# The order of a score tile and a product in the 64-row dense part of a fused attention and gated MLP kernel

## The chip, the cores and the metric

One Trainium2 chip, one of its cores. A core has TensorE (matmuls; PE in the profile, its weight loads are PEld), VectorE (DVE), ScalarE (ACT), GpSimd (POOL), SyncE (SP) and DMA queues; each engine works through its own queue, and they wait for each other by semaphores. TensorE writes to PSUM, which has eight banks; a matmul of 512 float32 columns fills one. The metric is the device time of one execution in microseconds (us), the median of some runs.

## What is computed

```python
xn = layernorm(x)                                   # x: 2048 x 512
q, k, v = xn @ wqkv, in 32 heads of 16
p = softmax(q @ k.T / 4)                            # per head, 2048 x 2048
s = (p @ v, heads joined) @ wo
g = silu(gelu(xn @ w1 + b1) @ w2 + b2)              # 512 -> 1376 -> 512
out = x + s * g
```

All in float32. The kernel gets float32 accuracy from the faster fp32r matmuls by splitting an operand into a high and a low part: a product is three matmuls, high x high, high x low and low x high.

## The kernel before

The program is one long, hand-ordered queue for each engine. It has three parts.

The first normalizes x, turns it, and makes the first columns of q, k and v.

The second is the **64-row dense part**. Here the remaining columns of q, k, v and all of the MLP are computed. Contractions of 128 rows are cut into two halves: a matmul takes rows 0 to 63 (row half 0) or 64 to 127 (row half 1) of its operands, and two matmuls of different halves can be in TensorE together. `run` (lines 593 to 600) gets two lists of such matmuls, one for each half, and queues them in pairs: `mm` (562 to 575, the matmul is at line 569) places one product of half `a`. An accumulation is begun by one half and ended by the other; `mark` (579 to 585, a tiny ACT or DVE copy) and the counters `prog`, `writer` and `seen` see to it that the second half begins on a bank only when the first is done.

In the same part **score tiles** are computed ahead of the attention, for the row maxima that the softmax needs: 128 queries against 512 keys of one head, a matmul of 48 rows on one row half (`s_mm`, line 190). `fill` (546 to 554) decides, before each product of half `a`, whether a score of that half goes in: when the half's count of matmuls, `row[a]`, has reached `due`, when it is that half's turn (`made`), and as long as fewer than 4 x LEAD = 604 have been placed. `due` grows by about three matmuls for each score, so that half 0 gets one, half 1 one three pairs later, half 0 the next two pairs after that: each half has a score and five products in turn. `taken` (556 to 560) counts the score.

A score takes one of two PSUM banks in turn (`s_ring`, line 91, and `s_tile`), and VectorE reads it with one maximum over each half of the 512 columns (`s_max`, line 195). So a score has to wait until the maximum of the score before the last has read its bank. When a block of 64 scores is done, `s_end0` (line 250) and `s_end1` (line 269) add a small maximum and a transpose on VectorE. The other banks hold accumulations of the dense part, which ACT empties (lines 363, 365, 382, 656).

The third part does the attention: transposed scores and exponentials (`t_one`), sums and products with v (`pv_step`), the rest of the score tiles (`s_op`), and at last the output projection and the gate.

What is queued where in the dense part is written out by `plan` (a list of dense halves and second-layer parts, made by due counts); each of its steps calls `run`. The order inside a pair is the loop in `run`, shown in the diff.

Of the kernel before, what the change touches and what calls it, by code (L numbers as in the profile page):

```python
# [49 lines left out]
def fused(ctx: ExitStack, tc: tile.TileContext, x, wqk, wv, wo, w1, b1, w2, b2, out):  # L50
# [115 lines left out]
    def tick():  # L166
        for e in later:
            e[0] -= 1
# [40 lines left out]
    def s_one(a):  # L209
        made[a] += 1  # L210
        s_whole(heads[made[a] - 1], a)
# [55 lines left out]
    def s_end1(u):  # L267
        mh = qring.tile([P, 2 * GH * NCH], F32, name="mh", bufs=1)
        nc.vector.transpose(mh, NM.pop(u).rearrange("p i a -> p (i a)").bitcast(F32))
        nc.sync.dma_start(mh_d[u].rearrange("i j (q b s) -> b (i j q) s", b=NCH, s=2 * GH * NCH), mh)  # L270
        sent.add(u)
# [274 lines left out]
    def fill(a):  # L546
        due = FILL0 + sum(made) * ROWS // (4 * LEAD)
        if sum(made) < 4 * LEAD and row[a] >= due and (made[0] <= made[1]) == (a == 0):
            taken()
            if later and later[0][0] <= 0:  # L550
                s_end1(later.pop(0)[1])
            s_one(a)
            row[a] += 1
            tick()

    def taken():
        prog["pe"] += 1
        s_when.append(prog["pe"])
        if len(s_when) > 2:
            prog["seen"] = max(prog["seen"], s_when[-3])  # L560

    def mm(a, key, ps, lhs, rhs, first, last):
        r = slice(64 * a, 64 * a + 64)
        token = None
        if not first and writer[key][0] != a and writer[key][1] > prog["seen"]:
            if not tokens or tokens[-1][0] < writer[key][1]:
                mark()
            prog["seen"], token = next(x for x in tokens if x[0] >= writer[key][1])
        i = nc.tensor.matmul(ps, lhs[r], rhs[r], start=first, stop=last).ins  # L569
        if token is not None:  # L570
            tc.add_manual_dep(i, token, SYNC, reason="other row tile")
        prog["pe"] += 1
        row[a] += 1
        latest[0] = (prog["pe"], i.name)
        writer[key] = (a, prog["pe"])
# [3 lines left out]
    def mark(dve=False):  # L579
        if dve:  # L580
            i = nc.vector.tensor_copy(junk[:, 1:], ident_r[:1, :1].bitcast(F32)).ins
        else:
            i = nc.scalar.activation(junk[:, :1], ident_r[:1, :1].bitcast(F32), AF.Copy).ins  # L583
        tc.add_manual_dep(i, latest[0][1], SYNC, reason="row tile done")
        tokens.append((latest[0][0], i.name))
# [7 lines left out]
    def run(ops, hooks={}):  # L593
        for n, two in enumerate(zip(*ops)):
            prog["n"] += 1
            for a in range(2):
                fill(a)
                mm(a, *two[a])
            for h in hooks.get(n, []):
                h()  # L600
# [25 lines left out]
    def down(c, f, part):  # L626
# [13 lines left out]
        if (c, f, part) == parts[-2]:  # L640
            run(ops, {2: [lambda: mark(True)], 5: [lambda: mark(True)]})
        else:
            run(ops, {3: [lambda: mark_early(n)]})
# [30 lines left out]
    def half(j, h):  # L674
        x, y = pairs[j]
        if h == 0:
            PH[x] = ps_x.tile([P, CH], F32, name="ps")
            PH[y] = ps_m.tile([P, CH], F32, name="ps")
            run((terms(x, 0, True), terms(y, 1, True)), {4: [lambda: w1_split(j + 1)], 8: [errand], 10: [chore]})
        else:  # L680
            run((terms(y, 0, False), terms(x, 1, False)), {2: [lambda: w1_load(j + 2), errand], 10: [chore]})
            evac((x, y), PH)
# [385 lines left out]
```

## Time and profile before

| what | value |
| --- | --- |
| median of 3 runs | 1564.38 us (1564.31 to 1565.07) |
| the profiled execution | 1565.26 us, its span 1563.2 us |
| first part, 0 to 41.66 us | PE busy 37.25, DVE 31.69, ACT 19.07 of 41.66 |
| dense part, 41.66 to 479.24 us | PE busy 437.58, DVE 395.19, ACT 167.71 of 437.58 |
| attention and output, 479.24 to the end | PE busy 1078.94, DVE 963.42, ACT 1055.35 of 1083.92 |
| granted TensorE clock | 1.00 in all three |

The span runs from the first to the last instruction of the program in the profile; the execution's own time is a little longer. A busy time is the time in which at least one instruction of the engine was running; two overlapping matmuls count once. In the prediction's fences, a timeline row gives start, length, engine, line, operation, tiles (written <- read) and shapes; L190 is a score, L569 a product, L195 the maximum that reads a score.

### The profile page before, as it was taken

What the parts mean: (1) busy time and instruction counts of PE and PEld (TensorE: products, weight loads), DVE (VectorE), ACT (ScalarE), POOL (GpSimd) and SP (SyncE); (2) the same over time, 40 slices, a digit from 0 to 9 for tenths busy, and PEclk for the clock granted to TensorE, in tenths of its full rate; (3) what the DMA queues carried; (4) which work ended last, traced back from release to release, by engine and by line L of the source; (5) the groups of instructions that cost most, each with busy time, mean ns of one, the idle gap of its engine ahead of it and who ended that gap; (6) DMA issues with size and microseconds to landing.
All of it is one profiled execution on the core that took longest, in us unless ns stands there. A gap on an engine that the chain in (4) does not pass through costs nothing.

```text
span 1563.2 us, 32584 instructions
## 1 busy us (share of the span) xinstructions
PE 1553.8 (99%) x12254; PEld 959.4 (61%) x12254; DVE 1390.3 (89%) x2306; ACT 1242.1 (79%) x2487; POOL 374.0 (24%) x392
## 2 busy tenths in 40 slices
PE   8999999999999999999999999999999999999998
PEld 7899999999995444444444444444444444444456
DVE  7899999999998999999999999999999999999833
ACT  4333343434348999999999999999999999999994
POOL 4135574755752000000000100010110000000144
PEclk9999999999999999999999999999999999999999
DMA  7515343356435011311110411141141111110153
GB/s 218 159 47 139 113 158 108 114 140 155 138 96 116 21 42 37 67 30 30 39 33 22 70 30 39 40 72 45 36 68 34 31 31 30 38 35 20 49 188 125
DMA packets 79501, 117.38 MB, mean 75 GB/s; under 512 B 28876, under 2 KB 29132, under 8 KB 77968
## 3 DMA queue, kind: packets, MB, share of 16 engines
q1 hardware_dynamic: 75884, 102.36, 23.7%
q0 software_dynamic: 2976, 12.35, 4.3%
q8 instruction: 97, 1.59, 0.4%
q10 hardware_dynamic: 484, 0.60, 0.1%
q14 instruction: 60, 0.49, 0.1%
HBM read 84.81 MB, written 25.97 MB: 71 GB/s over the span
## 4 chain that ended last, share of the span: by engine, by line
PE 98%; DVE 1%; DMA 1%; ACT 0%; issue 0%; ACTq 0%; SPq 0%
PE pv L800 32%; PE pst L737 15%; PE ps L737 14%; PE ps L569 13%; PE ps L190 10%; PE pst L569 7%; PE pv L569 3%; PE ps L917 2%; PE ps L450 1%; PE ps L81 1%; PE pst L81 1%; DVE st L411 0%; DMA xt<-in_x 0%; PE pst L434 0%; DVE slot L76 0%; DVE xn L425 0%
## 5 line engine op out<-in xcount | busy, mean ns | idle before, releaser
L195 DVE TENSOR_REDUCE mx<-ps 128x2 f32<-128x512 f32 x2048 | 1298.0, 685 | 108.1 <-PE ps L190 28.8
L739 ACT ACTIVATE slot<-pst 128x512 f32<-128x512 f32 x1533 | 804.2, 606 | 2.4 <-PE ps L190 1.5
L800 PE MATMUL pv<-slot,vsb 128*17 128x512 f32 (+1 forms) x4096 | 537.5, 598 | 0.2 <-DVE os L807 0.2
L190 PE MATMUL ps<-kt,slot 48*128 48x512 f32 x1350 | 382.7, 371 | 0.0
L739 ACT ACTIVATE slot<-ps 128x512 f32<-128x512 f32 x515 | 307.7, 598 | 5.4 <-PE ps L737 1.9
L737 PE MATMUL pst<-qt,kt 50*128 50x512 f32 x1149 | 304.8, 405 | 0.1
L737 PEld LDWEIGHTS ps<-qt,kt 50*128 50x128 f32 x387 | 70.8, 183 | 316.2 <-ACT slot L739 315.1
L190 PEld LDWEIGHTS ps<-kt,slot 48*128 48x128 f32 x1350 | 223.5, 184 | 4.1 <-DVE mx L195 0.5
L569 PE MATMUL ps<-slot,w1h 64*128 64x512 f32 x1104 | 222.7, 393 | 0.0
L737 PEld LDWEIGHTS pst<-qt,kt 50*128 50x128 f32 x1149 | 207.9, 185 | 21.9 <-DVE gt L654 1.2
L737 PE MATMUL ps<-qt,kt 50*128 50x512 f32 x387 | 190.1, 493 | 0.0
L190 PE MATMUL ps<-kt,qz 48*128 48x512 f32 x448 | 187.2, 418 | 0.0
L190 PE MATMUL ps<-slot,slot 48*128 48x512 f32 x584 | 168.7, 372 | 0.0
L569 PEld LDWEIGHTS ps<-slot,w1h 64*128 64x128 f32 x1104 | 156.2, 185 | 4.9 <-ACT junk L583 0.2
L569 PE MATMUL ps<-slot,w1l 64*128 64x512 f32 x552 | 145.8, 392 | 0.0
L370 POOL TENSOR_TENSOR hl<-hg,hh 128x512 fp32r<-128x512 f32 x76 | 96.8, 1295 | 134.2 <-ACT hh L369 108.8
L800 PEld LDWEIGHTS pv<-slot,vsb 128*17 128x17 f32 (+1 forms) x4096 | 69.8, 96 | 85.5 <-issue 33.3
L583 ACT ACTIVATE junk<-ident_r 1x1 f32<-1x1 f32 x94 | 18.4, 196 | 124.0 <-PE pst L569 112.5
L737 PE MATMUL pst<-qt,slot 50*128 50x512 f32 x384 | 99.7, 405 | 0.0
L190 PEld LDWEIGHTS ps<-slot,slot 48*128 48x128 f32 x584 | 97.3, 184 | 3.5 <-DVE mx L195 1.0
L837 POOL TENSOR_TENSOR slot<-slot,dn 64x512 f32<-64x512 f32 x16 | 20.5, 1282 | 315.5 <-PE pst L737 198.8
L190 PEld LDWEIGHTS ps<-kt,qz 48*128 48x128 f32 x448 | 82.1, 183 | 15.7 <-DVE mx L195 1.0
(153 smaller groups left out, 1744.7 us busy)
## 6 DMA issues: line engine op xcount, KB each, us to landing
raw<-in_w SPq DMA_DIRECT2D x88, 256.0 KB
qk_h<-hh SPq DMA_DIRECT2D x32, 256.0 KB
qk_l<-hl SPq DMA_DIRECT2D x32, 256.0 KB
qt<-qk_h SPq DMA_DIRECT2D x128, 64.0 KB
slot<-qk_h SPq DMA_DIRECT2D x92, 64.0 KB
g_d<-gt POOLq DMA_DIRECT2D x16, 256.0 KB, 3.1
qt<-qk_l SPq DMA_DIRECT2D x64, 64.0 KB
kt<-qk_h POOLq DMA_DIRECT2D x16, 256.0 KB, 6.3
```

The costliest lines, as they stand in the source:

```text
L81: nc.tensor.matmul(ps, lhs[a], rhs[b], start=first and n == 0, stop=last and n == 2)
L190: return nc.tensor.matmul(ps[:, c0:c0 + w], QS[u][r, p, qi * P:(qi + 1) * P], keys, start=True, stop=True).ins
L195: nc.vector.tensor_reduce(MX[u][:, 2 * p:2 * p + 2, qi, ki][:, heads, parts], ps.rearrange("p (n c) -> p n c", c=HC), axis=AX.X, op=OP.max)
L370: nc.gpsimd.tensor_sub(hl, raw, hh.bitcast(F32))
L450: nc.tensor.matmul(pq["q", g, c], W1[g][i][:, k * P:(k + 1) * P], (xh, xl)[j][c][:, k], start=n == 0 and k == 0, stop=n == 2 and k == KT - 1)
L569: i = nc.tensor.matmul(ps, lhs[r], rhs[r], start=first, stop=last).ins
L583: i = nc.scalar.activation(junk[:, :1], ident_r[:1, :1].bitcast(F32), AF.Copy).ins
L737: nc.tensor.matmul(ps, kts[KSET[g]][p][r, k * P:(k + 1) * P], QT[u][r, p, :], start=True, stop=True)
L739: nc.scalar.activation(PT[u, k][:, 2 * p + a, :], ps, AF.Exp, scale=SCALE)
L800: nc.tensor.matmul(PV[u][32 * j:32 * j + w, :], vsb[:, k, h:h + w], PT[u, k][:, j, :], start=(k == 0), stop=(k == NT - 1))
L837: eng.tensor_mul(ot[c][rs, g // 2], ot[c][rs, g // 2], DN.pop(u)[rs])
L917: op = nc.tensor.matmul(PW[b][0], OTS[b, k][i][r], (wo_h, wo_l)[j][r, k], start=part == 0 and n == 0, stop=part == 3 and n == 5).ins
```

## The change

In each pair of the dense part, both calls of `fill` now come ahead of both products. Before, the queue of TensorE had, for one pair: score of half 0 (if due), product of half 0, score of half 1 (if due), product of half 1. After, it has: score of half 0 (if due), score of half 1 (if due), product of half 0, product of half 1. For half 0 nothing moves; a score of half 1 goes one place ahead.

```diff
     def run(ops, hooks={}):
         for n, two in enumerate(zip(*ops)):
             prog["n"] += 1
             for a in range(2):
                 fill(a)
+            for a in range(2):
                 mm(a, *two[a])
             for h in hooks.get(n, []):
                 h()
```

## The prediction, made before the change was run

> **What bounds the kernel now.** I read the first page for the engines and the chain of waits.
>
> ```profile
> span 1563.2 us, 32584 instructions
> ...
> PE 98%; DVE 1%; DMA 1%; ACT 0%; issue 0%; ACTq 0%; SPq 0%
> ```
>
> 98% of the chain is TensorE's own work: time taken off or put on TensorE in one stage reaches the end. Then the dense part alone, in the table by stretches: first the instructions of the product line L569, then those of the score line L190 (columns: stretch, its length, TensorE busy and count, loads busy and count, granted clock, DMA share, GB/s).
>
> ```profile
> 41.66:479.24 437.58, 437.56 (x3072) 396.48 (x3072) 1.00 0.43 123
> ```
> ```profile
> 41.66:479.24 437.58, 252.64 (x604) 110.67 (x604) 1.00 0.43 123
> ```
>
> That is 3072 products and 604 scores (4 x LEAD, 302 on each half): 1838 slots for each half. The clock is full, and the products alone keep TensorE "busy" for 437.56 of 437.58 us, so small stalls must be looked for in the single instructions: two row halves overlap and hide them. The timeline of TensorE, then of TensorE and its loads, around 305 us (columns: start, length, engine, line, operation):
>
> ```profile
> 304.93 0.39 PE L569 MATMUL pv<-w2h,hl 64*128 64x512 f32 x1
> 305.01 0.39 PE L569 MATMUL pst<-w2h,hl 64*128 64x512 f32 x1
> 305.17 0.40 PE L190 MATMUL ps<-kt,qz 48*128 48x512 f32 x1
> 305.24 0.39 PE L569 MATMUL pst<-w2h,hh 64*128 64x512 f32 x1
> ```
> ```profile
> 305.01 0.19 PEld L569 LDWEIGHTS pst<-w2h,hh 64*128 64x128 f32 x1
> 305.04 0.18 PEld L190 LDWEIGHTS ps<-kt,qz 48*128 48x128 f32 x1
> ...
> 305.64 0.18 PEld L190 LDWEIGHTS ps<-kt,qz 48*128 48x128 f32 x1
> ...
> 305.69 0.44 PE L190 MATMUL ps<-kt,qz 48*128 48x512 f32 x1
> ```
>
> Here pv is row half 1 and pst is row half 0; the two run side by side, each at its own pace. Scores alternate: half 1's (call it S1) at 305.17, half 0's (S0) at 305.69. What does a slot cost when nothing holds it? A round, from S1 to S1, is six slots of a half (a score and five products). In one stretch the scores of half 1 are hardly held:
>
> ```profile
> 205.51 0.39 PE L190 MATMUL ps<-kt,qz 48*128 48x512 f32 x1
> ...
> 205.88 0.44 PE L190 MATMUL ps<-kt,qz 48*128 48x512 f32 x1
> ...
> 212.51 0.39 PE L190 MATMUL ps<-kt,qz 48*128 48x512 f32 x1
> ...
> 213.04 0.43 PE L190 MATMUL ps<-kt,qz 48*128 48x512 f32 x1
> ```
>
> S1 from 205.51 to 212.51 is five rounds: 7.00 / 30 = 0.233 a slot. Over all slots that do not follow a score, the starts in the trace give a mean of 0.2332 (half 0) and 0.2339 (half 1); I use 0.2335. The stage needs 1837 x 0.2335 = 428.9 us from its first to its last start, and takes 437.58 - 0.39 = 437.2. So **8.2 us are lost in stalls**. They sit behind the scores: the slot after an S0 lasts 0.262 in the mean, after an S1 0.258.
>
> Why do scores stall? Groups of the same stretch (busy us, mean ns of one, idle time before), and then the maxima of line 195, which read a score's bank, and what ended DVE's idle time ahead of them (us, times):
>
> ```profile
> L195 DVE TENSOR_REDUCE mx<-ps 128x2 f32<-128x512 f32 x604 | 389.9, 686 | 40.2 <-PE ps L569 8.7 <-PE pst L569 4.1 <-PE pv L569 2.1
> L569 PE MATMUL ps<-slot,w1h 64*128 64x512 f32 x1104 | 222.7, 393 | 0.0
> L190 PE MATMUL ps<-kt,qz 48*128 48x512 f32 x448 | 187.2, 418 | 0.0
> ```
> ```profile
> L195 DVE TENSOR_REDUCE mx<-ps x604: 647/691/695, 45.2 to 475.7; 128x2 f32<-128x512 f32 x151
> ...
>   PE ps L569: 8.7, 50
>   PE pst L569: 4.1, 23
>   PE pv L569: 2.1, 13
>   PE ps L190: 1.2, 4
> ```
>
> A score lasts 418 ns against a product's 393: its weights arrive late. Its load waits for one of two banks, and a bank comes free when DVE has read the score before the last. And DVE, when it is idle ahead of a maximum, is released 86 times by a *product* and 4 times by a score. Each maximum waits for its score and for what is queued just ahead of it. Two cases show it:
>
> ```profile
> 206.86 0.39 PE L569 MATMUL ps<-slot,w1h 64*128 64x512 f32 x1
> 206.91 0.40 PE L190 MATMUL ps<-kt,qz 48*128 48x512 f32 x1
> ```
> ```profile
> 207.35 0.69 DVE L195 TENSOR_REDUCE mx<-ps 128x2 f32<-128x512 f32 x1
> ```
> ```profile
> 304.30 0.69 DVE L195 TENSOR_REDUCE mx<-ps 128x2 f32<-128x512 f32 x1
> ```
> ```profile
> 304.90 0.68 DVE L195 TENSOR_REDUCE mx<-ps 128x2 f32<-128x512 f32 x1
> ```
> ```profile
> 305.69 0.69 DVE L195 TENSOR_REDUCE mx<-ps 128x2 f32<-128x512 f32 x1
> ```
>
> At 206.9 half 0's product (queued first) ended at 207.25, S1 at 207.31, and the maximum began 0.04 after S1. At 305.17 S1 ends at 305.57, but the product queued ahead of it begins after it, at 305.24, ends at 305.63, and the maximum starts only at 305.69: 0.12 after its own score. Over all 302 S1 the maximum starts 0.07 after that product's end (5th to 95th percentile 0.070 to 0.072), 0.17 after S1's own.
>
> This closes a loop, and it is what bounds the stage. Write R1, R0 for the maxima of S1, S0. R1 at 304.30; R0 at 304.90, when DVE takes the next (0.60); R0 ends at 305.58; the load of the next S0 in that bank at 305.64; S0 at 305.69, stretched by 0.05. So **R1 to S0 is 1.44**. Four slots later (0.93) half 0 starts the product ahead of the next S1, and R1 follows 0.39 + 0.07 after: 2.83 for two rounds, 1.42 a round. Measured: the 604 maxima start from 45.2 to 475.7, which is 430.5 us for 301.5 rounds, 1.428 a round, against 6 x 0.2335 = 1.401 for TensorE alone.
>
> **The change part by part.** The same instructions are queued. Whether `fill(1)` places a score depends on `row[1]` and `made`, which `mm(0)` does not touch, so all scores stay in their iterations; S0 and S1 never share one. In 302 iterations S1 goes ahead of half 0's product (M0) and not behind. The 96 marks of lines 581 and 583 stay 96, worked out from the counters of lines 546 to 589 in both orders. No DMA, no ACT, POOL or SP work moves; S0's place is unchanged.
>
> *Removed:* R1's wait for M0. What is queued ahead of S1 is then half 1's own last product, a slot earlier, done long before. R1 should start 0.04 after S1's end instead of 0.17: 0.13 sooner, 0.16 with S1's stretch of 0.025 gone.
>
> *Next in line:* R1's own bank: S1 to R1 0.43, R1 0.69, load 0.06, S1 at least 0.10 after (0.05 and a stretch of 0.05 at 305.64): 1.28 of 1.401, 0.12 to spare. S0: R1 to S0 still takes 1.44, so S0 can start effectively at S1 + 0.43 + 1.44 = 1.87; wanted is two slots and a round after that S1, 8 x 0.2335 = 1.868, plus the lag d of half 0 behind half 1. It fits if d is at least about 0.01. A late S0 itself makes d larger, and with M0 no longer in R1's way a larger d costs nothing. DVE takes a maximum each 0.60: 1.21 a round, not the bound. So rounds should come to six slots.
>
> *Added:* S1's wait now stands ahead of M0. Behind S1 on TensorE stand M0 and then half 1's next product; ACT waits for M0 only where M0 ends an accumulation. M0's load began at 305.01, as its predecessor started, and 0.23 ahead of its own start; S1's load, held, began at 305.04. Queued behind it, M0's load would still be up to 0.20 ahead, and a load needs about 0.10 (at 305.64: 0.05 and a stretch of 0.05). Cover 0.10 here, and more with S1's bank 0.16 sooner. Without it the cost is what is short, 302 times: from 0 to S1's own mean stretch, 302 x 0.025 = 7.6 us. I take 0, by the pair at 305.17.
>
> *Left over:* maxima of blocks and transposes sit between the scores' maxima:
>
> ```profile
> L250 DVE TENSOR_REDUCE nm<-mx 128x16 f32<-128x128 f32 x9 | 2.5, 275 | 0.0
> ...
> L269 DVE STREAM_TRANSPOSE mh<-nmh 128x32 f32<-128x32 f32 x9 | 1.8, 201 | 0.0
> ```
>
> Against 0.12 to spare they can hold S1 by 0.155 and 0.08: 0 to 9 x 0.235 = 2.1 us; I take 1.2. S0 has a spare of nearly 0 and slots vary by some ns: between 0 and half the rounds at today's excess of 0.026 (151 x 0.026 = 3.9); I take 0.5, since a larger d ends it.
>
> Sum: 8.2 - 1.2 - 0.5 = **6.5 us less**. The profiled execution took 1565.26 (span 1563.2 and 2.1 around it), 0.9 above the median of 1564.38; the saving is taken from the median: 1557.9. Later stages are the same queue and shift as they are.
>
> **One place where the skill speaks against it.** S1 at 305.17 is queued behind M0 at 305.24 and starts ahead of it: here the halves do not keep queue order between them. The Trainium skill (TensorE: Matmul & The Clock Gate, Part 3: Packing small matmuls, "The mechanism") says that matmuls are strictly first in, first out, in start and end. By that rule S1 would end last of the two, R1 would never wait for M0, nothing would be removed, and a held score would hold the other half: rival 3. Its sum would be nothing saved and up to 7.6 us lost, where the rows give 6.5 saved. The trace disagrees with it, by 0.07 us in this pair.
>
> **The rivals.**
> 1. *Part of it (16%).* S0's wait stays in many rounds. For it: in the stretch from 205.51 half 1 ran at full pace, yet half 0 did not. Its S0 went from 205.88 to 213.04 in five rounds, 1.432 each, until half 0 lagged enough. Against: that is just the growth of d, after which only today's order holds R1 again. If something resets d so often that half the rounds lose as now: 8.2 / 2 - 0.8 = 3.3 us less, 1561.1.
> 2. *Nothing (9%).* R1 waits, in the new order too, for whatever ends last in both halves, or S0's bank sets the round alone: 1564.4. Against: 206.86, where M0 ended first and R1 followed S1 by 0.04.
> 3. *Slower (7%).* The halves keep queue order where a score waits for its bank: M0 cannot start before the held S1 has started, so S1's stretch of 0.025 is lost by half 0 as well, on top of its own at S0. It decides where S1's load comes over 0.12 after its predecessor's start. 302 x 0.025 = 7.6 more: 1572.0. For: the loads of S1 are all late today. Against: the pair at 305.17.
>
> **How the numbers follow.** Forecast 68%, rivals 16, 9 and 7%. The time is the forecast's, 1557.9. Range: below, all 8.2 saved, 1556.2; above, the forecast and the larger part of rival 1 (2.4 saved), 1562.0. A measurement tells 0.2%, 3.1 us, from no change: the forecast and most of rival 1 (14 of 16) are faster, 82%; the rest and rival 2 within, 11%; rival 3 slower, 7%.
>
> **What would show it.** After the change, R1 starts 0.04 after S1's end; DVE's idle time ahead of line 195 is ended by line 190 and hardly by 569; scores last about 395 to 400 ns; a round is 1.40 to 1.41 and the dense part about 431. Wrong, if R1 still starts later than 0.10 after S1, if slots after S0 stay at 0.26, or if M0 comes more than 0.24 after its predecessor.

## The result and the profile after

The changed kernel takes 1557.55 us (1557.06 to 1557.83, 6 runs) against 1564.57 (1564.31 to 1565.07, 6 runs) for the kernel before beside it: 7.0 us less, a ratio of 0.9953 (95% interval 0.9943 to 0.9963). The forecast was 1557.9, 6.5 less. The profiled execution took 1557.83, its span 1555.7; before it was 1565.26 and 1563.2.

Where did the time come from? The table by stretches (all instructions; columns: stretch, its length, TensorE, loads, DVE, ACT and POOL busy with counts, granted clock, DMA share, GB/s). First the dense part of the kernel before, then that of the changed kernel and the rest of it:

```profile
41.66:479.24 437.58, 437.58 (x3686) 401.95 (x3689) 395.19 (x630) 167.71 (x373) 242.68 (x214) 1.00 0.43 123
```
```profile
41.66:471.98 430.32, 430.32 (x3686) 418.36 (x3689) 396.09 (x630) 168.22 (x373) 242.90 (x214) 1.00 0.44 125
471.98:1555.70 1083.72, 1078.80 (x8369) 524.87 (x8369) 962.74 (x1596) 1055.41 (x2076) 113.76 (x153) 1.00 0.21 50
```

The counts of the dense part are those of before. It took 437.58 and takes 430.32: 7.26 less. The first part still ends at 41.66, and attention and output take 1083.72 against 1083.92. All of the gain lies in the dense part. DVE, ACT and POOL have the same work as before, within 1 us.

The groups of this stretch, and what ended DVE's idle time ahead of the maxima, for the changed kernel:

```profile
L195 DVE TENSOR_REDUCE mx<-ps 128x2 f32<-128x512 f32 x604 | 391.0, 686 | 31.9 <-PE ps L190 2.9
L569 PE MATMUL ps<-slot,w1h 64*128 64x512 f32 x1104 | 217.8, 392 | 0.0
L190 PE MATMUL ps<-kt,qz 48*128 48x512 f32 x448 | 176.2, 394 | 0.0
```
```profile
L195 DVE TENSOR_REDUCE mx<-ps x604: 647/690/694, 45.3 to 468.3; 128x2 f32<-128x512 f32 x151
...
  PE ps L190: 2.9, 9
```

Before, products ended that idle time 86 times and scores 4 times; now scores do it 9 times and products never (only waits long enough for the view are counted). A score lasts 394 ns and not 418, as short as a product: its weights are there. The maxima now run from 45.3 to 468.3, 423.0 us for 301.5 rounds: 1.403 a round, where it was 1.428 and TensorE alone needs 1.401. One pair of the changed kernel, and the maximum that follows:

```profile
300.75 0.39 PE L569 MATMUL pv<-w2h,hl 64*128 64x512 f32 x1
300.85 0.39 PE L569 MATMUL pst<-w2h,hl 64*128 64x512 f32 x1
300.98 0.40 PE L190 MATMUL ps<-kt,qz 48*128 48x512 f32 x1
301.08 0.39 PE L569 MATMUL pst<-w2h,hh 64*128 64x512 f32 x1
```
```profile
301.41 0.69 DVE L195 TENSOR_REDUCE mx<-ps 128x2 f32<-128x512 f32 x1
```

S1 at 300.98 follows half 1's product of 300.75 after 0.23, without a hold, and ends at 301.37. R1 starts at 301.41, before M0 (301.08) ends at 301.47. Over all S1, R1 starts 0.040 after S1's end; before it was 0.171.

### The profile page after: what moved, and what is told of

Its sections match the earlier page's. It is cut to its first block, busy times and chain, and to the rows that moved or that the text cites. A ratio compares the mean times of both kernels' runs of the same rounds, so it can differ in the third digit from the quotient of the medians.

```text
span 1555.7 us, 32584 instructions
## 1 busy us (share of the span) xinstructions
PE 1546.0 (99%) x12254; PEld 974.3 (63%) x12254; DVE 1390.5 (89%) x2306; ACT 1242.7 (80%) x2487; POOL 374.4 (24%) x392
## 4 chain that ended last, share of the span: by engine, by line
PE 97%; DVE 1%; ACT 1%; DMA 0%; issue 0%; ACTq 0%
PE pv L801 32%; PE pst L738 14%; PE ps L738 14%; PE ps L569 13%; PE ps L190 10%; PE pst L569 7%; PE pv L569 3%; PE ps L918 2%; ACT slot L740 1%; PE ps L450 1%; PE ps L81 1%; PE pst L81 1%; DVE st L411 0%; DMA xt<-in_x 0%; PE pst L434 0%; DVE slot L76 0%
## 5 line engine op out<-in xcount | busy, mean ns | idle before, releaser
L569 PE MATMUL ps<-slot,w1h 64*128 64x512 f32 x1104 | 217.8, 392 | 0.0
L190 PE MATMUL ps<-kt,qz 48*128 48x512 f32 x448 | 176.2, 394 | 0.0
L569 PEld LDWEIGHTS ps<-slot,w1h 64*128 64x128 f32 x1104 | 152.1, 185 | 3.7 <-ACT junk L583 0.2
L569 PE MATMUL ps<-slot,w1l 64*128 64x512 f32 x552 | 139.7, 392 | 0.0
L738 PEld LDWEIGHTS ps<-qt,slot 50*128 50x128 f32 x128 | 23.4, 183 | 108.8 <-ACT slot L740 108.8
```

The lines of the kernel that those rows point to most:

```text
L190: return nc.tensor.matmul(ps[:, c0:c0 + w], QS[u][r, p, qi * P:(qi + 1) * P], keys, start=True, stop=True).ins
L738: nc.tensor.matmul(ps, kts[KSET[g]][p][r, k * P:(k + 1) * P], QT[u][r, p, :], start=True, stop=True)
```

## The experiments

Theory A is the prediction's: R1 waits for M0, half 0's product queued ahead of S1, and this closes a loop R1, R0, S0, M0, R1 over two rounds; the change opens it. Rivals are named in the expectations. Twelve kernels ran, in three groups; each group has its own runs of the kernel before beside it.

| kernel | median us | before beside it | ratio (95% interval) | dense part us |
| --- | --- | --- | --- | --- |
| the change | 1557.55 | 1564.57 | 0.9953 (0.9943 to 0.9963) | 430.32 |
| e1_wait | 1560.58 | 1565.51 | 0.9970 (0.9958 to 0.9981) | 433.62 |
| e2_late_max | 1558.01 | 1565.51 | 0.9952 (0.9940 to 0.9965) | 430.30 |
| e3_even | 1558.52 | 1565.51 | 0.9956 (0.9943 to 0.9968) | 431.11 |
| e7_mirror | 1558.45 | 1565.51 | 0.9957 (0.9944 to 0.9971) | 430.65 |
| e10_lag | 1558.61 | 1564.80 | 0.9960 (0.9948 to 0.9973) | 431.18 |
| e11_wait_lag | 1568.04 | 1564.80 | 1.0019 (1.0010 to 1.0028) | 440.83 |
| e8_even_after | 1557.48 | 1564.80 | 0.9953 (0.9939 to 0.9966) | 429.93 |
| e9_lead | 1565.47 | 1564.80 | 1.0008 (0.9999 to 1.0017) | 437.39 |
| e4_half | 1563.82 | 1565.10 | 0.9991 (0.9982 to 1.0000) | 436.86 |
| e12_pairs | 1561.60 | 1565.10 | 0.9978 (0.9969 to 0.9987) | 434.13 |
| e5_short_before | 1557.59 | 1565.10 | 0.9951 (0.9938 to 0.9963) | 429.84 |
| e6_short_after | 1557.35 | 1565.10 | 0.9950 (0.9937 to 0.9962) | 429.86 |

### e1_wait and e2_late_max: the new order, with and without the wait

```diff
             for a in range(2):
                 mm(a, *two[a])
+                while held:
+                    s_max(*held.pop(), latest[0][1])
```
```diff
-    def s_max(ps, job, heads, parts):
+    def s_max(ps, job, heads, parts, behind=None):
...
+        if behind is not None:
+            tc.add_manual_dep(red.ins, behind, SYNC, reason="product behind the score")
```

`held` has the score of half 1 whose maximum is put off; `latest[0][1]` names M0, just queued. e2_late_max is the same without this second argument.

e1_wait:

> The queue of TensorE as after the change (S1 ahead of M0), but the maximum R1 of each S1 in the dense part is made to wait for M0 as well, the product queued just behind S1. Theory A (the gain is R1's freedom from M0's end: R1 at S1's end + 0.04 and not at M0's end + 0.07, which breaks the loop R1, R0, S0, M0): the wait is back, so the round is about 1.42 to 1.43 again, the slots behind S0 about 0.26, the dense part about 437 us, the time 1564.5, within 1.5. Rival B (the gain is S1's earlier place in the queue: its bank wait and its load are met sooner): S1 keeps its place, so 1557.5, the dense part 430.

e2_late_max:

> The control of e1_wait: the maximum of each S1 is issued at the same later place of the program, but waits for nothing more than its score. Theory A and rival B alike: as after the change, 1557.5, within 1, R1 0.04 after S1's end. If it is slower, the later issue of the maximum and not its wait would explain e1_wait.

e2_late_max came out as expected, so the later issue costs nothing. e1_wait lost 2.6 of the 7.5 us, not all of them. The time lies between the numbers of theory A and rival B and fits neither. One score of e1_wait (TensorE, then the maximum that reads it):

```profile
299.91 0.45 PE L576 MATMUL ps<-slot,w1h 64*128 64x512 f32 x2
300.15 0.39 PE L190 MATMUL ps<-kt,qz 48*128 48x512 f32 x1
300.20 0.39 PE L576 MATMUL ps<-slot,w1l 64*128 64x512 f32 x1
```
```profile
300.63 0.69 DVE L195 TENSOR_REDUCE mx<-ps 128x2 f32<-128x512 f32 x1
```

S1 ends at 300.54, M0 (the row at 300.20) at 300.59, R1 starts at 300.63: the wait for M0 is there. But over all scores, where R1 waits for M0 it starts 0.037 after M0's end, and in the kernel before 0.071 (the last section shows where the difference comes from). So I had put back a wait that is 0.034 shorter, and the loop as the prediction counts it is then 2.83 - 0.034 = 2.80 for two rounds, 1.40 each: level with TensorE's own 1.401. The loop was just on the edge. Its maxima came 1.414 a round apart, so this count leaves 0.01 a round unexplained. Whether the 2.6 us, and not 7, mean this or an advantage of the place itself, this pair could not say; e10 and e11 were made for it.

### e10_lag and e11_wait_lag: the same lag, with and without half 0

```diff
+            lag = nc.vector.tensor_copy(lags[0], ident_r[:1, :1].bitcast(F32)).ins
+            tc.add_manual_dep(lag, behind, SYNC, reason="lag")
```

The copy stands ahead of R1 on DVE; `behind` is S1 in e10_lag and M0 in e11_wait_lag.

e10_lag:

> As e2_late_max (after the change, the maximum of S1 issued a little later), but a one-element copy on DVE, which waits for S1, stands ahead of each R1 in the dense part: R1 is late by a fixed lag L behind S1's end, 0.06 to 0.14 us by the copies of line 581, and still does not depend on M0. Theory A (only a lateness of R1 that comes from half 0 feeds back): half 0 falls back once, by L, and then loses nothing; S1's own bank has 0.12 to spare: 1558.0, within 1.5, as long as L stays under 0.12. Rival D (R1's lateness costs as such, whatever it waits for; before the change it was 0.13): L / 0.13 of the 7.3 us, so 1561.4 for 0.06 and 1565.5 for 0.14.

e11_wait_lag:

> As e10_lag, but the copy waits for M0 (the product queued behind S1) and not for S1: R1 starts at M0's end + 0.04 + L. Theory A: the loop R1, R0, S0, M0, R1 takes 2.80 + L for two rounds, so each round is L / 2 longer than in e1_wait, which had 1560.6: 1560.6 + 151 x L = 1569.7 for L = 0.06, 1581.7 for 0.14. Rival D: e10_lag plus what the wait cost in e1_wait (2.6): 1564 to 1568. If e11_wait_lag lies no further from e10_lag than e1_wait lay from e2_late_max, the loop is wrong.

The groups of the dense part, e10_lag and then e11_wait_lag:

```profile
L190 PE MATMUL ps<-kt,qz 48*128 48x512 f32 x448 | 177.5, 396 | 0.0
...
L196 DVE COPY lag<-ident_r 1x1 f32<-1x1 f32 x302 | 42.8, 142 | 18.8 <-PE ps L190 1.6
```
```profile
L190 PE MATMUL ps<-kt,qz 48*128 48x512 f32 x448 | 190.3, 425 | 0.0
...
L196 DVE COPY lag<-ident_r 1x1 f32<-1x1 f32 x302 | 42.8, 142 | 28.5 <-PE ps L577 1.5 <-PE ps L190 1.0 <-PE pst L577 0.7
```

A copy lasts 142 ns, but the next maximum starts 0.07 after it: in e10_lag R1 is 0.110 behind S1's end and not 0.040. L is 0.07. The same lag makes the dense part 0.9 us longer than that of e2_late_max if it hangs on S1 (rival D wanted 7.3 x 0.07 / 0.13 = 3.9), and 10.5 us longer if it hangs on M0. Scores are stretched only in the second (425 against 396 ns). From the loop: 2.80 + 0.07 for two rounds is 1.435 a round; the 10.5 us over 302 rounds give 1.403 + 0.035 = 1.438. My expectation of 1571.2 for this L (1560.6 + 151 x 0.07) was 3.2 too high: it added the whole of L to e1_wait, whose 1.414 a round already lay above the 1.40 of its loop. In e11_wait_lag R1 starts 0.580 after S1's start, in the kernel before 0.587; yet it is slower than before, because here the lag comes on top of M0's end. For the lag of 0.07 that was tried, **it is not how late R1 is that costs, but on what its lateness hangs.** The 1568.04 lies at the upper end of the range put on rival D (1564 to 1568), but that range counted on an e10_lag of 1561 or more. By rival D's own rule, the measured e10_lag and 2.6 give 1561.2. The two runs lie 9.4 apart, where e1_wait and e2_late_max lay 2.6 apart. Rival D falls.

### e4_half and e12_pairs: half of the scores set ahead

```diff
+            if made[1] % 2:
+                fill(0)
+                fill(1)
+                mm(0, *two[0])
+                mm(1, *two[1])
+            else:
+                for a in range(2):
+                    fill(a)
+                    mm(a, *two[a])
```

This is e4_half; e12_pairs has `made[1] // 2 % 2` for the condition.

e4_half:

> Every second S1 of the dense part goes ahead of M0 (151 of 302), the others stay behind it. Theory A, taken at its word: the loop runs over two rounds, from an R1 that waited for M0 to the S0 of the next round, to M0, to the R1 after that. With every second S1 changed one of the two interlaced loops stays closed; holds of S0 in two rounds running must still add up to what they add up to today, so the rounds stay at 1.42: 1564.8 less at most 1.5. Rival E (each S1 set ahead gives its own share): half the gain, 1561.3, within 0.8.

e12_pairs:

> The same number of S1 (150 or 152 of 302) goes ahead of M0, but in turns of two: two rounds with S1 ahead, two with S1 behind. Theory A: both loops are now cut every second time they go round; one hold of S0 in four rounds takes the place of two: half the gain or a little more, 1560.5 to 1561.8. Rival E: half, 1561.3, as e4_half. The two runs together tell: A wants e4_half at least 2 us above e12_pairs, E wants them equal.

Both set half of the S1 ahead, one by one or two by two: 1.3 us less (the interval of its ratio just reaches 1) and 3.5 us less, in one group of runs; the dense part 436.86 and 434.13. Rival E falls: a score set ahead has no gain of its own. In e4_half what ended DVE's idle time ahead of the maxima is still a product, 137 times; in e12_pairs, 67 times:

```profile
  PE ps L569: 19.5, 74
  PE pst L569: 13.0, 52
  PE pv L569: 2.9, 11
  PE ps L190: 2.4, 7
```
```profile
  PE ps L569: 9.3, 36
  PE pst L569: 6.3, 24
  PE pv L569: 1.8, 7
  PE ps L190: 1.6, 4
```

That the loop spans two rounds, so that every second open link does next to nothing, was a consequence that no other theory named here has.

### e3_even, e7_mirror and e8_even_after: other places for the scores

```diff
-        if sum(made) < 4 * LEAD and row[a] >= due and (made[0] <= made[1]) == (a == 0):
+        if sum(made) < 4 * LEAD and row[a] >= due - a and (made[0] <= made[1]) == (a == 0):
```
```diff
-            for a in range(2):
+            for a in (1, 0):
                 fill(a)
                 mm(a, *two[a])
```

The first is e3_even (in the kernel before) and e8_even_after (in the changed kernel), the second is e7_mirror (in the kernel before).

e3_even:

> The order before the change (S1 behind M0), but S1 is due one pair sooner, so that S0 and S1 stand three slots apart in both directions and not four and two. Theory A: R1 still waits for M0 (M0's end + 0.07), but S0 now comes 0.70 + d after S1 and not 0.47 + d, so R0 is no longer held behind R1 (R1 + 0.61 = S1 + 1.07 + d; S0 + 0.43 = S1 + 1.13 + d), the loop is open, rounds come to 1.40 to 1.41 although R1 is late: 1557.5, within 1.5. Rival B, and anyone who holds that S1's place behind M0 costs as such: 1564.5.

e7_mirror:

> The order before the change with the halves exchanged inside each pair: score of half 1 if due, product of half 1, score of half 0 if due, product of half 0. S1 then follows half 0's product of the pair before, done a slot earlier, and S0 stands behind half 1's product M1 of its own pair. Theory A: R1 is free (S1's end + 0.04); R0 waits for M1, which ends no later than S1 + 0.93, and R0 must wait for DVE until R1 + 0.61 = S1 + 1.04 in any case: no new wait, 1557.5, within 1.5. Rival C (a score queued behind the other half's product of its own pair costs as such, whichever half it is): 1564.5.

e8_even_after:

> Both cures at once: the order after the change, and S1 due one pair sooner, three slots from S0 on both sides. Theory A: R1 and R0 each start 0.04 after their scores' ends and DVE holds neither; but the loop was open with either cure alone, and the rounds are at 1.403 against 1.401 for TensorE, so there is nothing left to win: ratio to before 0.9953, within 0.0006 (1558.0 beside 1565.5). If gains added up, 1551 to 1554.

Maxima and scores of e3_even in its dense part:

```profile
L195 DVE TENSOR_REDUCE mx<-ps 128x2 f32<-128x512 f32 x604 | 411.0, 691 | 12.4 <-PE ps L190 1.8 <-PE pst L569 0.3
...
L190 PE MATMUL ps<-kt,qz 48*128 48x512 f32 x448 | 176.4, 394 | 0.0
```

In e3_even S1 stands behind M0 as before, and the gain is there: 0.9956, with scores of 394 ns as in the changed kernel. R1 still waits for M0 (it starts 0.071 after M0's end in 229 of 302 rounds), though it is less late, 0.086 behind S1's end in the mean and not 0.171. Scores are 0.69 to 0.71 apart, R0 comes 0.70 after R1 and not 0.61, and the loop is open at that link. Rival B, for which the place ahead of M0 counts, falls. e7_mirror gives 0.9957, so rival C falls too; but the exchange moved the scores to 0.69 and 0.71 apart as well, which I had not expected, so it does not show more than e3_even does. e8_even_after, with both cures, is level with the change: the gains do not add up.

### e5_short_before and e6_short_after: shorter maxima

```diff
-        nc.vector.tensor_reduce(MX[u][:, 2 * p:2 * p + 2, qi, ki][:, heads, parts], ps.rearrange("p (n c) -> p n c", c=HC), axis=AX.X, op=OP.max)
+        nc.vector.tensor_reduce(MX[u][:, 2 * p:2 * p + 2, qi, ki][:, heads, parts], ps.rearrange("p (n c) -> p n c", c=HC)[:, :, ::2 if "seen" in prog else 1], axis=AX.X, op=OP.max)
...
-        nc.scalar.activation(PT[u, k][:, 2 * p + a, :], ps, AF.Exp, scale=SCALE)
+        nc.scalar.activation(PT[u, k][:, 2 * p + a, :], ps, AF.Exp, scale=SCALE / 16)
```

e5_short_before:

> The order before the change, but in the dense part each maximum reads every second column of its score (256 of 512), and the exponentials of the attention have a smaller scale, so that wrong maxima overflow nowhere: row maxima and output are not the reference's. Theory A: R1 still waits for M0, but R0 follows R1 sooner and each maximum is about 0.27 shorter, so R1 to S0 falls from 1.44 to about 0.9 and the loop is open: 1558.0, within 1. Rival F (R1's wait for M0 costs as such, or the place of S1 does): 1564.8.

e6_short_after:

> The order after the change with the same shorter maxima and the same smaller scale (row maxima and output are not the reference's). All theories: no faster than after the change by over 1, 1557.5; it shows what the shorter maxima alone do, and is to be set against e5_short_before.

In the old order the shorter maxima alone bring the whole gain (0.9951), and in the new order they bring nothing more (0.9950). Maxima and scores of e5_short_before, then the maxima of e6_short_after:

```profile
L195 DVE TENSOR_REDUCE mx<-ps 128x2 f32<-128x256 f32 x604 | 256.5, 425 | 164.8 <-PE ps L190 73.9 <-PE ps L569 41.9 <-PE pst L569 27.6
...
L190 PE MATMUL ps<-kt,qz 48*128 48x512 f32 x448 | 171.9, 392 | 0.0
```
```profile
L195 DVE TENSOR_REDUCE mx<-ps 128x2 f32<-128x256 f32 x604 | 256.6, 425 | 164.4 <-PE ps L190 145.0 <-PE pst L569 1.2
```

DVE waits here for products for at least 41.9 + 27.6 = 69.5 us, against 14.9 in the kernel before, and the kernel is 7.5 us faster. The wait for M0 that the change removes is harmless as soon as the rest of the loop is short: rival F falls, and this row is the plainest warning against reading a cost off a column of waits.

### e9_lead: more scores in the dense part

```diff
-LEAD = 151
+LEAD = 155
```

> After the change, with LEAD 155 in place of 151: 16 score tiles move from the attention into the dense part. If the dense part is bound by TensorE's slots now, it grows by 8 x 0.2335 = 1.9 us, and the attention, where TensorE is the bound too, loses 16 scores of 0.12 to 0.2 us: 1556.5 to 1558.2 beside 1565.5. If DVE or the two banks bound the dense part, it grows by 8 x 1.40 = 11 us and the time is about 1566.

1565.47: the first case of my expectation is wrong; the second has the time about right, but not the growth of the dense part. The dense part, then the rest of e9_lead:

```profile
41.74:479.13 437.39, 436.94 (x3072) 390.90 (x3072) 1.00 0.43 123
```
```profile
479.13:1563.50 1084.37, 1079.19 (x8347) 523.06 (x8347) 953.71 (x1580) 1055.42 (x2076) 113.69 (x153) 1.00 0.22 50
```

The dense part grew by 7.1 us, not by 1.9 and not by 11, and the attention, with 16 scores less, is not shorter (1084.4 against 1083.7), ACT's 1055.4 being unchanged. With 310 scores a half, 37 of the rounds of half 0 and 36 of half 1 have five slots, 1.17 us, under the 1.28 that S1's own bank takes by the prediction's count. 73 scores last over 0.45 us, against 7 in the changed kernel, and 70 of the 73 end such a round; the slot behind a score that ends one lasts 0.33, behind any other score 0.235. So the loss stands at the short rounds (5.2 us over 37 is 0.14 each). That the bank alone makes it was not tried apart.

## Why the prediction was right

**What bounds the dense part** stands: the stalls behind the scores, 8.2 us by its count. Now the slot after an S0 lasts 0.236 and after an S1 0.234 (0.262 and 0.258 before), and 430.32 - 0.39 - 428.9 = 1.0 us is left of them.

**R1's wait for M0, removed.** R1 moved to 0.040 after S1's end, as forecast (0.04). e10 against e11 shows that the dependence on half 0 is what costs, e3 and e5 that it costs nothing once another link of the loop is short.

**The loop of two rounds.** It was argued from one example; e4 against e12 shows its length, e11 its rate. Its margin is thin: 1.42 against 1.40, and the count comes out 0.003 to 0.014 a round under what was measured (1.42 for 1.428, 1.40 for 1.414 in e1_wait, 1.435 for 1.438 in e11_wait_lag).

**S0 next in line, with a lag d of at least 0.01.** In the changed kernel M0 starts 0.087 after S1 in the mean (5th to 95th percentile 0.014 to 0.164), so half 0 keeps far enough behind without any help. R0 is still taken by DVE 0.61 after R1.

**The added wait ahead of M0 at no cost.** S1's load now starts 0.018 after its predecessor product starts, in the mean, and 0.22 ahead of S1, so there is hardly a hold to pass on; M0 starts 0.233 after its own predecessor. The slower rival needs held scores, and e11_wait_lag has them in the new order: where S1's load started over 0.17 after its predecessor product (83 rounds), the slot behind S1 lasts 0.289, but M0, queued behind S1, starts 0.234 after its predecessor, and the slot behind M0 lasts 0.245. So a hold of S1 costs the other half 0.01 and not its full length, and the halves do not keep queue order here either.

**What was off** is a size: the left-over. The prediction kept back 1.2 for block maxima and transposes and 0.5 for slots that vary; all of it together is 1.0. Stretches of 18 slots around those instructions lose hardly more than others, under 0.2 us in all on either half, so the 1.2 was too much. The stage saved 7.26 and not 6.5, the medians 7.0. The partial rival (1561.1) did not come: the stretch around 205 us was, as the argument against it said, only the growth of d.

## What to carry to other kernels

When a stage runs a few per cent behind an engine that looks busy, look for the loop: follow one wait from engine to engine until it comes back, add its parts and set them against the engine's own pace for as many rounds as the loop spans. A wait costs what the loop is longer than that pace, not its own length, and any link may be shortened: here the queue order, the spacing of the scores and the length of the maxima each brought the same 7 us, and two together no more. And where a consumer waits for one matmul, see what is queued just ahead of it, since here it waited for that as well.

## What the runs showed of the hardware

Matmuls of the two row halves start out of queue order (S1 0.07 before M0 in the prediction's pair, and so in most rounds before), but the maximum was released in queue order: with M0 queued ahead and ending later, R1 starts 0.071 after M0's end (5th to 95th percentile 0.070 to 0.072), and 0.037 after the end of the matmul that it waits for when nothing ahead ends later. The 0.034 between them is what was missing in e1_wait.

The trace has the times at which semaphores were raised, and they show the step. In the kernel before, M0 and S1 both raise the semaphore that R1 waits for. Where S1 ended over 0.04 ahead of M0 (283 of 302 rounds), nothing is raised at S1's end: the semaphore goes up 0.014 and 0.048 after M0's end, and R1 starts 0.023 after the second. In the changed kernel it goes up 0.014 after S1's end, and R1 starts 0.024 later. In e1_wait 271 of the 302 S1 raise nothing of their own, so that one step is left. The Trainium skill (TensorE: Matmul & The Clock Gate, Part 3, "The cost: per-tile semaphore tail") says that completion increments of concurrent matmuls are written one after another, about 26 ns each; two increments in a row, M0's and then S1's, would give such a step. Here two in a row stand 0.034 apart and not 0.026. Whether S1 would be seen at its own end if it raised a semaphore that M0 does not raise, no run here shows.

A one-element DVE copy lasts 142 ns, but holds the next maximum by only 70; a maximum over 512 columns lasts 686 ns and holds the next by 608.
